# A transformed convolution on one core: other places for two weight loads, another order of the first unit, other copy costs

## The chip, the cores and the metric

The kernel runs on 1 core of one Trainium2 chip. The metric is the device time of one execution in microseconds; the number of a kernel is the median of its runs. TensorE (PE) multiplies, VectorE (DVE) and ScalarE (ACT) read and write PSUM and SBUF, GpSimd (POOL) works on SBUF, and SyncE (SP) issues nearly all transfers on one queue.

## The reference

A convolution along the sequence with three taps, an affine step per output channel, and SiLU. All tensors are bf16.

```python
B, S, C = 2, 2048, 1024          # x: (B, S, C); w: (3, C, C); mean, var, g, b: (C,)
xp = jnp.pad(x, ((0, 0), (1, 1), (0, 0)))
y = sum(jnp.einsum('bsc,cd->bsd', xp[:, k:k + S, :], w[k]) for k in range(3))
y = (y - mean) * (g / jnp.sqrt(var + 1e-5)) + b
return y * sigmoid(y)
```

## The kernel before

Instead of three taps for each row, the kernel uses a transform that gives 6 output rows from 8 input rows with 8 products ("points" 0 to 7). 2048 rows make 342 tiles of 6.

**Input.** The rows of a batch come in 17 windows of 21 tiles (127 or 128 rows, the last one of 33). `load_window` (L203) fetches a window; its tiles are in a pool of 10 buffers, `xwin`, save for the first window of each batch, which has the buffer `xw0`. `transform` (L216) multiplies a window on TensorE with the transform matrix `Rm`, one matmul for each of the 8 blocks of 128 input channels, and copies the result from PSUM to the bf16 tensor `T_sb[batch]`, laid out by channel block, point and tile. In batch 0 a copy holds 4 blocks (672 elements for each partition); in batch 1 a window makes three groups of 3, 3 and 2 blocks (504, 504 and 336), each in one of the PSUM banks 4 to 7 in turn. Each copy goes to ScalarE or VectorE, whichever has less in the running account `load`; `EVAC` (L175) gives a copy's price on each as a fixed part and a part for each block.

**Weights.** They come in 8 chunks of 128 output channels. Points 0 and 7 use the raw taps 0 and 2. The weights of points 1 to 6 are the tensor `uch`, made on GpSimd: `scale_weights` (L142) makes the scaled taps `w2x`, `w1x`, `w0x`; `pair_sum` (L156) adds the outer taps, with `n` = 0, 1, 2 for three weightings; `pair_tap` (L169) adds the middle tap to such a sum or subtracts it from it, for points 1, 3, 5 and 2, 4, 6. So `pair_sum` needs taps 0 and 2 alone, and every `pair_tap` needs tap 1. For chunks 2 to 7, ScalarE does the scaling and VectorE the first sum (`outer_by_reduce`); chunks 2 to 7 come in pairs by `load_weights` (L82), chunks 0 and 1 tap by tap by `load_chunk` (L87), 256 KB each in runs of 256 bytes.

**Units.** A unit (`unit`, L258) is one chunk for one batch: 64 matmuls of 342 columns, 8 for each point, into four banks. bA takes points 1, 2 and 0, bB 3 and 4, bC 5 and 6, bG 7. Points that share a bank accumulate, with copies of the partial sums between them (`copy_out` on ScalarE: m1, m3, s1, s2, m5) and combining steps on VectorE (`stt`, L279). A later point of a bank can't start until the copy of the earlier one is made. Three activations (`silu`) end the unit; they are put off into the next one by the list `late`, and are called from `copy_out`. The order of points is 1, 3, 2, 4, 5, 7, 6, 0; in the first unit, with `seven_first`, it is 7, 1, 3, 2, 4, 5, 0, 6.

**Order.** It is written out by hand: each engine runs its instructions in program order. The loop at L344 runs the windows of batch 0, with the taps of chunk 0 issued behind window 3 (tap 0), 5 (tap 2) and 13 (tap 1), and GpSimd's work for chunk 0 at windows 7 and 13. The loop at L366 runs the windows of batch 1, with chunk 1's taps issued at window 10, and spreads the first 52 matmuls of the first unit (chunk 0, batch 0) between its 51 groups. Then come the rest of the first unit and the other units, with the weights of the next chunk made during the second unit of the chunk before it (L425 to L439). For chunk 1, GpSimd also makes `w2x` (L431). SyncE issues in this order as well.

Of the kernel before, what the change touches and what calls it, by code (L numbers as in the profile page):

```python
# [9 lines left out]
ALU = mybir.AluOpType  # L10
# [25 lines left out]
def kernel(  # L36
# [45 lines left out]
    def load_weights(dp):  # L82
        open_weights(dp)
        for k in (0, 2, 1):
            nc.sync.dma_start(out=pair_tile[dp][:, k], in_=w_all[:, k, :, dp * 2 * P:(dp + 1) * 2 * P])

    def load_chunk(dc, k):  # L87
        nc.sync.dma_start(out=raw[dc][k], in_=w_all[:, k, :, dc * P:(dc + 1) * P])  # L88
# [53 lines left out]
    def scale_weights(dc, taps=(2, 1, 0), on_gpsimd=False):  # L142
        for k in taps:
            f = 2.0 if k == 1 else 4.0
            dst = wx[dc, k] = wtmp.tile([P, CT, P], BF16, name=f"w{k}x")
            if on_gpsimd:
                nc.gpsimd.tensor_scalar(dst, raw[dc][k], f, 0.0, op0=ALU.mult, op1=ALU.add)
            else:
                nc.scalar.mul(dst, raw[dc][k], f)

    def open_chunk(dc):
        wts[dc] = upool.tile([P, 6, CT, P], BF16, name="uch")
# [3 lines left out]
    def pair_sum(dc, n, engine=nc.gpsimd):  # L156

        e = outer[dc, n] = wtmp.tile([P, CT, P], FP32, name=("e1", "e2", "eh")[n])
        a = wx[dc, 0] if n == 2 else raw[dc][0]
        c = wx[dc, 2] if n == 1 else raw[dc][2]  # L160
        engine.tensor_tensor(e, a, c, op=ALU.add)  # L161
# [7 lines left out]
    def pair_tap(dc, n, op):  # L169
        odd = wx[dc, 1] if n else raw[dc][1]  # L170
        nc.gpsimd.tensor_tensor(wts[dc][:, 2 * n + (op == ALU.subtract)], outer[dc, n], odd, op=op)  # L171

    T_sb = [tpool.tile([P, CT, NJ, NTB], BF16, name=f"T_sb{bi}") for bi in range(B)]
    load = {"act": 0.0, "dve": 1.0}
    EVAC = {"act": (0.17, 0.14), "dve": (0.12, 0.17)}  # L175

    sk = consts.tile([P, DC], FP32, name="sk")
    beta = consts.tile([P, DC], FP32, name="beta")
# [59 lines left out]
        else:  # L238
            nc.vector.tensor_copy(dst, src)  # L239

    def mms(bk, j, dc, bi, c0, c1, start):

        for ct in range(CT):
            if j in (0, 7):
                lhsT = raw[dc][0 if j == 0 else 2][:, ct, :]
            else:
                lhsT = wts[dc][:, j - 1, ct, :]
            nc.tensor.matmul(  # L248
                ps_all[:, bk * 512:bk * 512 + c1 - c0],
                lhsT=lhsT,  # L250
                rhs=T_sb[bi][:, ct, j, c0:c1],
                start=start and ct == 0,
                stop=ct == CT - 1,
                skip_group_check=not start,
            )
            yield

    def unit(dc, bi, c0, c1, banks, yT, late, pace=(1, 0, 1, 1, 0), seven_first=False):  # L258

        nn = c1 - c0
        A, B_, C_, G = [ps_all[:, k * 512:k * 512 + nn] for k in banks]
        bA, bB, bC, bG = banks
        pace = list(pace)  # L270

        def et(name):
            return epool.tile([P, NTB], FP32, name=name)[:, 0:nn]

        m1, m3, m5, s1, s2, d1 = (et(n) for n in ("m1", "m3", "m5", "s1", "s2", "d1"))
        y_all = epool.tile([P, M_OUT, NTB], FP32, name="y")[:, :, 0:nn]
        y = [y_all[:, i] for i in range(M_OUT)]

        def stt(o, i0, s, i1, op1=ALU.add):  # L279
            nc.vector.scalar_tensor_tensor(out=o, in0=i0, scalar=s, in1=i1, op0=ALU.mult, op1=op1)  # L280
            load["dve"] += 0.0013 * nn

        def copy_out(dst, src):
            for _ in range(pace.pop(0)):
                if late:
                    late.pop(0)()
            nc.scalar.copy(dst, src)  # L287
            load["act"] += 0.0013 * nn

        if seven_first:  # L290
            yield from mms(bG, 7, dc, bi, c0, c1, True)
        yield from mms(bA, 1, dc, bi, c0, c1, True)
        copy_out(m1, A)
        yield from mms(bB, 3, dc, bi, c0, c1, True)
        copy_out(m3, B_)
        yield from mms(bA, 2, dc, bi, c0, c1, False)
        copy_out(s1, A)
        stt(d1, m1, 2.0, A, op1=ALU.subtract)
        yield from mms(bB, 4, dc, bi, c0, c1, False)
        copy_out(s2, B_)  # L300
        for i in (2, 4):
            stt(y[i], B_, ALPHA * 2.0 ** i, s1)
        stt(B_, m3, 2.0, B_, op1=ALU.subtract)
        yield from mms(bC, 5, dc, bi, c0, c1, True)
        copy_out(m5, C_)
        while late:
            late.pop(0)()
        for i in (1, 3, 5):
            stt(y[i], B_, ALPHA * 2.0 ** i, d1)
        yield from mms(*((bA, 0) if seven_first else (bG, 7)), dc, bi, c0, c1, not seven_first)  # L310
        nc.vector.tensor_tensor(y[5], G, y[5], op=ALU.add)  # L311
        yield from mms(bC, 6, dc, bi, c0, c1, False)
        for i in (2, 4):
            stt(y[i], C_, BETA * 0.5 ** i, y[i])
        stt(G, m5, 2.0, C_, op1=ALU.subtract)
        if not seven_first:
            yield from mms(bA, 0, dc, bi, c0, c1, False)
        for i in (1, 3, 5):
            stt(y[i], G, BETA * 0.5 ** i, y[i])
        stt(y[0], s2, ALPHA, A)  # L320
        stt(y[0], C_, BETA, y[0])

        def silu(i0, i1):
            nc.scalar.activation(  # L324
                yT[:, i0:i1:2, c0:c1],
                y_all[:, i0:i1:2],
                ACT.Silu,
                bias=beta[:, dc:dc + 1],
                scale=sk[:, dc:dc + 1],
            )  # L330

        late.extend(lambda i=i: silu(*i) for i in ((2, 5), (1, 6), (0, 1)))
# [10 lines left out]
    with tc.tile_pool(name="xwin", bufs=10) as xpool:  # L343
        for wi in range(NWIN):  # L344
            window = load_window(xpool, 0, wi)
            if wi in (3, 5, 13):
                load_chunk(0, {3: 0, 5: 2, 13: 1}[wi])
            for h in range(2):
                transform(0, wi, window, 4 * h, 4, (2 * wi + h) % 4 * 2, 2)
            if wi == 0:  # L350
                turn_params()
            if wi == 7:
                open_chunk(0)
                for n, taps in ((0, ()), (1, (2,)), (2, (0,))):
                    scale_weights(0, taps, on_gpsimd=True)
                    pair_sum(0, n)
            if wi == 13:
                pair_tap(0, 0, ALU.add)
                scale_weights(0, (1,), on_gpsimd=True)
                for n, op in ((1, ALU.add), (0, ALU.subtract), (1, ALU.subtract), (2, ALU.add), (2, ALU.subtract)):  # L360
                    pair_tap(0, n, op)
        make_params()
        first = unit(0, 0, 0, NTB, (0, 1, 2, 3), yTs[0], late, seven_first=True)
        load["act"] = load["dve"] = 0.0
        gi, done = 0, 0
        for wi in range(NWIN):  # L366
            window = load_window(xpool, 1, wi)
            if wi == 10:
                for k in (0, 2, 1):
                    load_chunk(1, k)  # L370
            for ct0, n in ((0, 3), (3, 3), (6, 2)):
                transform(1, wi, window, ct0, n, 4 + gi % 4, 3)
                gi += 1
                want = 52 * max(gi - 1, 0) // (3 * NWIN - 1)
                run(first, want - done)
                done = want
        load_weights(1)
        run(first)

# [40 lines left out]
    for ui, (dc, bi) in enumerate(units[1:-1], 1):  # L420
        yT = yTs[ui % 2]
        half = 4 * (ui % 2)
        if bi == 0 and dc + 1 < DC:
            outer_by_reduce(dc + 1)
        if bi == 1 and dc + 1 < DC:  # L425
            open_chunk(dc + 1)
            if dc == 0:
                pair_sum(1, 0)
                for op in (ALU.add, ALU.subtract):
                    pair_tap(1, 0, op)  # L430
                scale_weights(1, (2,), on_gpsimd=True)  # L431
                scale_weights(1, (1, 0))
            else:
                scale_weights(dc + 1)
            for n in range(0 if dc else 1, 3):
                if n:
                    pair_sum(dc + 1, n)
                for op in (ALU.add, ALU.subtract):
                    pair_tap(dc + 1, n, op)  # L439
        run(unit(dc, bi, 0, NTB, (half, half + 1, half + 2, half + 3), yT, late))  # L440
        if ui < len(units) - 2:
            late.append(lambda dc=dc, bi=bi, yT=yT: finish(dc, bi, yT))
        if bi == 1 and dc % 2 == 1 and (dc + 3) // 2 < DC // 2:
            load_weights((dc + 3) // 2)
# [87 lines left out]
```

## Time and profile before

| | us |
|---|---|
| median of 3 runs | 194.63 |
| lowest and highest run | 193.66, 194.88 |
| profiled execution | 193.69 |
| its span | 191.8 |
| TensorE busy | 178.5 |
| VectorE busy | 161.7 |
| GpSimd busy | 147.9 |
| ScalarE busy | 123.3 |

All times in views are microseconds from the start of the span. A row of the timeline gives start, length, engine, line, operation, what it writes and reads, the count, and in brackets the idle time of the engine before it and what ended it. Such rows overlap a little, since instructions are pipelined. In a table of stretches each engine has its busy time with the number of its instructions. The granted TensorE clock is 0.989 over the span.

The groups of batch 1's stage, 21.5 to 39.5 us, that matter here, with the mean length of one (ns):

| engine, line, what | count | mean ns |
|---|---|---|
| ACT L237 copy of 504 | 17 | 605 |
| ACT L237 copy of 336 | 7 | 453 |
| DVE L239 copy of 504 | 15 | 682 |
| DVE L239 copy of 336 | 9 | 506 |
| DVE L280 combining step (y<-ps_all,s) | 2 | 509 |
| ACT L287 copy out of a bank (m<-ps_all) | 3 | 450 |
| POOL L171 weights of a point | 8 | 2127 to 2134 |
| POOL L147 scaling of a tap | 1 | 1037 |

### The profile page before, as it was taken

The numbers are of one execution on the slowest core, as the hardware profiler recorded it, in microseconds if no ns is written. First come the engines' busy times: TensorE is split into PE (matmuls) and PEld (weight loads), VectorE is DVE, ScalarE is ACT, GpSimd is POOL, SyncE is SP. The second block draws the span as 40 slices with busy tenths as digits, with TensorE's granted clock in tenths as the row PEclk, the third lists the DMA queues.
The fourth block names the chain that finished last, engine by engine and source line by source line (L and its number), as shares of the span: only waits on it lengthen the run. The fifth ranks groups of instructions, "written<-read, shape, count | busy, mean of one in ns | idle before, by whom it ended". The sixth has DMA issues, their size and how long they took to land.

```text
span 191.8 us, 3900 instructions
## 1 busy us (share of the span) xinstructions
PE 178.5 (93%) x1404; PEld 125.2 (65%) x1404; DVE 161.7 (84%) x344; ACT 123.3 (64%) x206; POOL 147.9 (77%) x89
## 2 busy tenths in 40 slices
PE   7877799999999999999999999999999999999840
PEld 3666688866666666666666666666666666679830
DVE  6579898987999699969996998799789969697880
ACT  3778588878278628764874587368727782727940
POOL 6379999999949996999699969987997899600000
PEclk9999999999999999999999999999999999999995
DMA  5999999960609398998374699676474738285604
GB/s 133 311 373 316 363 274 241 288 151 8 115 19 190 63 200 224 198 200 174 75 162 87 155 286 214 134 156 123 112 137 96 151 87 164 69 178 122 153 6 109
DMA packets 86759, 31.72 MB, mean 165 GB/s; under 512 B 73364, under 2 KB 82580, under 8 KB 86740
## 3 DMA queue, kind: packets, MB, share of 16 engines
q1 hardware_dynamic: 86637, 31.46, 70.0%
q8 instruction: 11, 0.18, 0.4%
q14 instruction: 8, 0.07, 0.1%
q10 hardware_dynamic: 103, 0.02, 0.0%
HBM read 14.82 MB, written 8.39 MB: 121 GB/s over the span
## 4 chain that ended last, share of the span: by engine, by line
PE 78%; DMA 10%; DVE 5%; ACT 2%; issue 1%; SPq 0%; DVEq 0%; ACTq 0%
PE ps_all L248 74%; DMA xw<-in_x_dram 10%; PE ps_all L223 5%; DVE y L280 3%; ACT yT L324 1%; DVE T_sb L239 1%; DVE o_end L490 1%; DVE ps_all L280 0%; ACT s L287 0%; DVE y L311 0%; DVE o_end L498 0%; ACT m L287 0%; SPq L88 0%; PE ps_all L458 0%; DVEq L490 0%
## 5 line engine op out<-in xcount | busy, mean ns | idle before, releaser
L248 PE MATMUL ps_all<-T_sb,uch 128*128 128x342 bf16 (+2 forms) x816 | 123.4, 299 | 1.1 <-ACT m L287 1.1
L248 PEld LDWEIGHTS <-uch 128*128 128x128 bf16 x816 | 76.6, 97 | 34.9 <-issue 1.5
L324 ACT ACTIVATE yT<-y,beta,sk 128x684 bf16<-128x684 f32 (+8 forms) x51 | 47.1, 926 | 32.0 <-DVE y L280 31.9
L280 DVE SCALAR_TENSOR_TENSOR y<-ps_all,y 128x342 f32<-128x342 f32 (+2 forms) x102 | 45.4, 486 | 1.8 <-PE ps_all L248 0.7
L248 PE MATMUL ps_all<-T_sb,wch 128*128 128x342 bf16 (+2 forms) x272 | 44.1, 299 | 0.0
L171 POOL TENSOR_TENSOR uch<-e,wch 128x1024 bf16<-128x1024 f32 x16 | 33.8, 2133 | 10.5 <-PE ps_all L248 5.6
L171 POOL TENSOR_TENSOR uch<-e,w1x 128x1024 bf16<-128x1024 f32 x16 | 33.8, 2132 | 0.6
L171 POOL TENSOR_TENSOR uch<-eh,w1x 128x1024 bf16<-128x1024 f32 x16 | 33.8, 2134 | 0.5
L287 ACT COPY m<-ps_all 128x342 f32<-128x342 f32 (+2 forms) x51 | 21.6, 425 | 19.6 <-PE ps_all L248 18.9
L223 PE MATMUL ps_all<-Rm,xw 128*128 128x168 bf16 (+1 forms) x272 | 29.7, 238 | 4.1 <-DMA xw<-in_x_dram 3.7
L248 PEld LDWEIGHTS <-wch 128*128 128x128 bf16 x272 | 25.6, 97 | 11.2
L237 ACT CAST T_sb<-ps_all 128x672 bf16<-128x672 f32 (+5 forms) x45 | 26.0, 606 | 8.4 <-PE ps_all L223 7.5
L239 DVE CAST T_sb<-ps_all 128x672 bf16<-128x672 f32 (+3 forms) x40 | 26.4, 698 | 4.0 <-PE ps_all L223 3.5
L223 PEld LDWEIGHTS <-xw 128*128 128x128 bf16 (+1 forms) x272 | 22.2, 100 | 10.1 <-DMA xw<-in_x_dram 5.2
L280 DVE SCALAR_TENSOR_TENSOR y<-ps_all,d 128x342 f32<-128x342 f32 (+2 forms) x51 | 22.0, 485 | 0.6
L280 DVE SCALAR_TENSOR_TENSOR y<-ps_all,s 128x342 f32<-128x342 f32 (+2 forms) x34 | 15.1, 487 | 4.0 <-ACT s L287 4.0
L161 POOL TENSOR_TENSOR e<-wch,w2x 128x1024 f32<-128x1024 bf16 x8 | 17.0, 2126 | 0.2
L161 POOL TENSOR_TENSOR eh<-w0x,wch 128x1024 f32<-128x1024 bf16 x8 | 17.0, 2128 | 0.1
L280 DVE SCALAR_TENSOR_TENSOR d<-m,ps_all 128x342 f32<-128x342 f32 (+2 forms) x17 | 8.3, 487 | 10.4 <-ACT s L287 10.4
L280 DVE SCALAR_TENSOR_TENSOR ps_all<-m,ps_all 128x342 f32<-128x342 f32 (+2 forms) x34 | 16.6, 487 | 0.0
L287 ACT COPY s<-ps_all 128x342 f32<-128x342 f32 (+2 forms) x34 | 14.2, 419 | 0.0
L167 DVE TENSOR_REDUCE e<-wch 128x1024 f32<-128x2048 bf16 x6 | 13.7, 2278 | 0.0
(44 smaller groups left out, 70.2 us busy)
## 6 DMA issues: line engine op xcount, KB each, us to landing
xw<-in_x_dram SPq DMA_DIRECT2D x30, 256.0 KB
out_dram<-o_sb SPq DMA_DIRECT2D x28, 192.0 KB
wch<-in_w_dram SPq DMA_DIRECT2D x9, 512.0 KB
out_dram<-o_sb SPq DMA_DIRECT2D x14, 120.0 KB
wch<-in_w_dram SPq DMA_DIRECT2D x6, 256.0 KB
xw<-in_x_dram SPq DMA_DIRECT2D x2, 224.0 KB
out_dram<-o_before SPq DMA_DIRECT2D x2, 192.0 KB
o_sb<-yT SPq DMA_TRANSPOSE x14
```

The costliest lines, as they stand in the source:

```text
L161: engine.tensor_tensor(e, a, c, op=ALU.add)
L167: nc.vector.tensor_reduce(e, taps.rearrange("p k ct d -> p ct d k"), axis=mybir.AxisListType.X, op=ALU.add)
L171: nc.gpsimd.tensor_tensor(wts[dc][:, 2 * n + (op == ALU.subtract)], outer[dc, n], odd, op=op)
L223: nc.tensor.matmul(banks[:, at:at + NJ * ntile], lhsT=xw[0:kk, (ct0 + c) * P:(ct0 + c + 1) * P], rhs=Rm[0:kk, :, 0:ntile], start=True, sto ...
L237: nc.scalar.copy(dst, src)
L239: nc.vector.tensor_copy(dst, src)
L248: nc.tensor.matmul(ps_all[:, bk * 512:bk * 512 + c1 - c0], lhsT=lhsT, rhs=T_sb[bi][:, ct, j, c0:c1], start=start and ct == 0, stop=ct == C ...
L280: nc.vector.scalar_tensor_tensor(out=o, in0=i0, scalar=s, in1=i1, op0=ALU.mult, op1=op1)
L287: nc.scalar.copy(dst, src)
L324: nc.scalar.activation(yT[:, i0:i1:2, c0:c1], y_all[:, i0:i1:2], ACT.Silu, bias=beta[:, dc:dc + 1], scale=sk[:, dc:dc + 1],)
L490: nc.vector.tensor_copy(ends[k][0:n1 - n0], pv[0:n1 - n0])
```

## The change

It has four parts, all before the third unit.

- The taps of chunk 0 are issued elsewhere on SyncE's queue: tap 2 behind window 6, tap 0 behind window 10, tap 1 behind the last window of batch 0. GpSimd's work for chunk 0 stands in one piece, in the order w2x, sum 0, sum 1, w0x, point 1, w1x, points 3, 2, 4, sum 2, points 5, 6. It is the same 12 instructions.
- The first unit's order is 0, four of the eight matmuls of 7, then 1, 3, 2, 4, 5, the other four of 7, and 6. The first 12 of its matmuls run before the windows of batch 1, and 40 are spread between the groups. Point 0 starts bank A, so points 1 and 2 accumulate on it: ScalarE copies out m0 and a0 instead of s1 and s2, and VectorE takes m0 off again in two combining steps (s1 and A) that were not there. `y[0]` gets its part of point 0 earlier. VectorE has two instructions more in this unit and ScalarE's copies are as many as before.
- Chunk 1's taps are issued behind all windows of batch 1. Its `w2x` is made by ScalarE, not GpSimd.
- The prices of `EVAC` have smaller fixed parts. By the account that follows from them, ScalarE gets 19 copies of 504 (or their short ones) and 10 of 336 in batch 1, VectorE 15 and 7; before, it was 19 and 8 against 15 and 9.

```diff
-    EVAC = {"act": (0.17, 0.14), "dve": (0.12, 0.17)}
+    EVAC = {"act": (0.09, 0.14), "dve": (0.085, 0.17)}
...
-        if seven_first:
-            yield from mms(bG, 7, dc, bi, c0, c1, True)
-        yield from mms(bA, 1, dc, bi, c0, c1, True)
-        copy_out(m1, A)
+        if not zero_first:
+            yield from mms(bA, 1, dc, bi, c0, c1, True)
+            copy_out(m1, A)
+        else:
+            m0, a0 = et("m0"), s2
+            yield from mms(bA, 0, dc, bi, c0, c1, True)
+            copy_out(m0, A)
+            yield from mms(bG, 7, dc, bi, c0, c1, True, range(CT // 2))
+            yield from mms(bA, 1, dc, bi, c0, c1, False)
+            copy_out(m1, A)
         yield from mms(bB, 3, dc, bi, c0, c1, True)
         copy_out(m3, B_)
         yield from mms(bA, 2, dc, bi, c0, c1, False)
-        copy_out(s1, A)
+        if not zero_first:
+            copy_out(s1, A)
+        else:
+            copy_out(a0, A)
+            stt(s1, A, 1.0, m0, op1=ALU.subtract)
+            stt(A, A, 1.0, m0)
         stt(d1, m1, 2.0, A, op1=ALU.subtract)
         yield from mms(bB, 4, dc, bi, c0, c1, False)
-        copy_out(s2, B_)
+        if not zero_first:
+            copy_out(s2, B_)
+        else:
+            stt(y[0], B_, ALPHA, a0)
...
-        yield from mms(*((bA, 0) if seven_first else (bG, 7)), dc, bi, c0, c1, not seven_first)
+        yield from mms(bG, 7, dc, bi, c0, c1, not zero_first, range(CT // 2 if zero_first else 0, CT))
...
-            if wi in (3, 5, 13):
-                load_chunk(0, {3: 0, 5: 2, 13: 1}[wi])
+            if wi in (6, 10, NWIN - 1):
+                load_chunk(0, {6: 2, 10: 0, NWIN - 1: 1}[wi])
...
-            if wi == 7:
-                open_chunk(0)
-                for n, taps in ((0, ()), (1, (2,)), (2, (0,))):
-                    scale_weights(0, taps, on_gpsimd=True)
-                    pair_sum(0, n)
-            if wi == 13:
-                pair_tap(0, 0, ALU.add)
-                scale_weights(0, (1,), on_gpsimd=True)
-                for n, op in ((1, ALU.add), (0, ALU.subtract), (1, ALU.subtract), (2, ALU.add), (2, ALU.subtract)):
-                    pair_tap(0, n, op)
+        open_chunk(0)
+        scale_weights(0, (2,), on_gpsimd=True)
+        pair_sum(0, 0)
+        pair_sum(0, 1)
+        scale_weights(0, (0,), on_gpsimd=True)
+        pair_tap(0, 0, ALU.add)
+        scale_weights(0, (1,), on_gpsimd=True)
+        pair_tap(0, 1, ALU.add)
+        for n in (0, 1):
+            pair_tap(0, n, ALU.subtract)
+        pair_sum(0, 2)
+        for op in (ALU.add, ALU.subtract):
+            pair_tap(0, 2, op)
         make_params()
-        first = unit(0, 0, 0, NTB, (0, 1, 2, 3), yTs[0], late, seven_first=True)
+        first = unit(0, 0, 0, NTB, (0, 1, 2, 3), yTs[0], late, zero_first=True)
         load["act"] = load["dve"] = 0.0
-        gi, done = 0, 0
+        gi, done = 0, 12
+        run(first, done)
         for wi in range(NWIN):
             window = load_window(xpool, 1, wi)
-            if wi == 10:
-                for k in (0, 2, 1):
-                    load_chunk(1, k)
             for ct0, n in ((0, 3), (3, 3), (6, 2)):
                 transform(1, wi, window, ct0, n, 4 + gi % 4, 3)
                 gi += 1
-                want = 52 * max(gi - 1, 0) // (3 * NWIN - 1)
+                want = 12 + 40 * max(gi - 1, 0) // (3 * NWIN - 1)
                 run(first, want - done)
                 done = want
+        for k in (0, 2, 1):
+            load_chunk(1, k)
         load_weights(1)
         run(first)
...
-                scale_weights(1, (2,), on_gpsimd=True)
-                scale_weights(1, (1, 0))
+                scale_weights(1)
```

## The prediction

> **What bounds the kernel now.** I read the page first (share of each engine, the 40 slices), then the chain of waits, then TensorE's, GpSimd's and ScalarE's rows in order of time for the first 45 us, and the table of stretches for the DMA rates.
>
> ```profile
> span 191.8 us, 3900 instructions
> ...
> PE 178.5 (93%) x1404; PEld 125.2 (65%) x1404; DVE 161.7 (84%) x344; ACT 123.3 (64%) x206; POOL 147.9 (77%) x89
> ...
> PE   7877799999999999999999999999999999999840
> ...
> PE 78%; DMA 10%; DVE 5%; ACT 2%; issue 1%; SPq 0%; DVEq 0%; ACTq 0%
> ```
>
> TensorE is full from the sixth slice (24 us) to the tail; only the first five slices have room. So the change is worth what it takes from the time before TensorE is full, less any new wait behind it. The rows of TensorE show the edges of that stretch:
>
> ```profile
> 11.41 5.97 PE L223 MATMUL ps_all<-Rm,xw 128*128 128x168 bf16 x64 [1.00 <-DMA xw<-in_x_dram]
> 18.04 0.75 PE L223 MATMUL ps_all<-Rm,xw 128*128 128x168 bf16 x8 [0.66 <-DMA xw<-in_x_dram]
> 19.12 1.08 PE L223 MATMUL ps_all<-Rm,xw 128*128 128x168 bf16 x16 [0.32 <-DMA xw<-in_x_dram]
> 21.50 0.59 PE L223 MATMUL ps_all<-Rm,xw 128*128 128x168 bf16 x6 [1.30 <-DMA xw<-in_x_dram]
> ```
>
> The first batch is through at 20.20; then 1.30 us of idling until batch 1's first window lands (the chain has that transfer from 14.78 for 6.59 us: landed at 21.37). Two rates of the queue, and the stage after it (last columns: clock, DMA share, GB/s):
>
> ```profile
> 10.50:14.50 4.00, 3.02 (x35) 2.59 (x36) 2.91 (x4) 2.98 (x5) 3.51 (x3) 1.00 1.05 387
> 26.00:29.00 3.00, 3.00 (x36) 2.57 (x34) 2.81 (x5) 2.57 (x6) 3.00 (x2) 1.00 1.06 217
> 21.50:39.50 18.00, 17.90 (x188) 14.73 (x189) 16.25 (x32) 15.13 (x33) 17.84 (x10) 1.00 1.03 285
> ```
>
> In 10.5 to 14.5 x rows travel alone: a window of 128 rows (262 KB) takes 0.68 us at 387 GB/s. In 26 to 29 it is mostly chunk 1's taps: the same bytes take 1.2 us at 217. A tap ahead of the windows costs 1.2 us of queue.
>
> **Before, in fixed points.** S = 21.50: batch 1's windows begin. E = 39.51: its 136 transform matmuls and 52 of the unit's 64 are done (row at 39.22, two more of 0.145). X = 43.77: the second unit's third tap starts, after a wait for ScalarE's copy; from there the chain is TensorE without a break (31.23 us for 214 matmuls), so any shift of X goes through to the end. The stage S to E is 18.0 us. Its work: 128 transforms in threes of 0.22 (9.3) and 8 short ones (0.4), 52 matmuls of 0.145 (7.5), together 17.2; 0.8 is stalls, mainly these VectorE pieces of the chain:
>
> ```profile
> 35.63 0.68 DVE T_sb L239
> 36.31 0.85 DVE y L280 x2
> ```
>
> **Part 1: middle tap behind batch 0, first 12 matmuls ahead of batch 1.** With 1.2 us less in the queue the first batch is through at about 19.0; it cannot come before 18.0, because the copies set 0.75 us a window (5.97 us for eight) from 5.98 on. The 12 matmuls need its last copy (before: last copy at 21.03, 0.83 after TensorE; I take 0.7), so they run from 19.7 to 21.4 (12 x 0.145). The bytes ahead of batch 1's first window are the same as before, only in another order, so it still lands at about 21.4 and S stays 21.5, now with 12 matmuls done in what was idling: 1.74 us. If the first batch gains nothing, they end at 22.7 and 1.2 of this is lost.
>
> The Trainium skill ("DMA: Bandwidth & Descriptors", section "Why small descriptors are slow") charges a 256-byte descriptor 3 cycles on 8; a tap would then cost about 0.9 us, an estimate from that page, against the 1.2 of the rows. By it the 12 matmuls end at 21.7 instead of 21.4, still before the wait of part 2, and the sum is the same.
>
> **Part 2: GpSimd's chain starts later.** This is the new wait. Its rows now:
>
> ```profile
> 10.84 2.12 POOL L161 TENSOR_TENSOR e<-wch 128x1024 f32<-128x1024 bf16 x1 [2.78 <-DMA wch<-in_w_dram]
> ...
> 19.56 2.12 POOL L171 TENSOR_TENSOR uch<-e,wch 128x1024 bf16<-128x1024 f32 x1
> 21.65 1.04 POOL L147 TENSOR_SCALAR w1x<-wch 128x1024 bf16<-128x1024 bf16 x1
> 22.77 2.13 POOL L171 TENSOR_TENSOR uch<-e,w1x 128x1024 bf16<-128x1024 f32 x1
> ```
>
> The steps are 2.09 (tensor) and 1.12 (scale). Everything from the first weight of point 1 on needs the middle tap, which lands at L. Batch 1's first window is behind it (0.67 us), so L is at most 20.7. The last window of batch 0 had landed by 19.1 to 19.9; without the tap ahead 17.9 to 18.7, and 1.2 for the tap gives 19.1 to 19.9 as the lower end. I take 20.4, nearer the upper end, since the queue's total is what the trace shows. Then point 1's weights are ready at L+2.1 = 22.5, while TensorE is there at 21.5 + three groups (0.6) = 22.1: a wait of 0.4, with the windows queued behind it on TensorE. Point 3's are ready at L+5.3 = 25.7; TensorE comes at 22.5 + 8 x 0.145 + 10 groups of 0.193 = 25.6. Points 2, 4 and 5 (L+7.4, L+9.5, L+13.8, the sum with four more tensor steps and a pair sum) are ready at 27.8, 29.9, 34.2, before TensorE at 28.8, 31.9, 35.0. What is left after 25.7: 32 matmuls (4.6) and 38 groups, three of them short (7.2): E would be 37.5.
>
> **Part 3: the copies.** Back-to-back instructions overlap by 0.09 (two of VectorE's 0.51 in 0.93). By that the stage holds on VectorE 15 copies of 504 (0.59), 7 of 336 (0.42) and 7 combining steps (0.42) = 14.7; on ScalarE 19 (0.52), 10 (0.36) and 3 unit copies (0.36) = 14.6. The two extra combining steps (s1 and A) and the new weights of the copies are in that. Before it was 14.3 and 14.6 in 18.0 us; now it has to fit in 16. The bursts of three and four steps on VectorE hold copies behind them, and four banks are all the room. Bounds: no stall, or, with full durations and no overlap (17.4 us), E = 39.9, 2.4 more. I take 0.5, below the 0.8 of before, as the cost weights move copies off VectorE just there. E = 38.0.
>
> **Part 4: chunk 1's weights behind batch 1, its scaling on ScalarE.** The three taps no longer stand before windows 11 to 16; the 0.15 us late matmul at 32.83 goes. They are issued when batch 1's sixth window frees its buffer (about 28) and land by 33.5; GpSimd wants them at L+15.9 = 36.3, so their later place costs nothing. ScalarE now has three scalings where it had two:
>
> ```profile
> 39.46 1.06 ACT L149 ACTIVATE w1x<-wch 128x1024 bf16<-128x1024 bf16 x1
> 40.42 1.05 ACT L149 ACTIVATE w0x<-wch 128x1024 bf16<-128x1024 bf16 x1
> 42.43 0.96 ACT L324 ACTIVATE yT<-y,beta,sk 128x684 bf16<-128x684 f32 x1 [0.97 <-DVE y L280]
> 43.30 0.99 ACT L287 COPY m<-ps_all 128x342 f32<-128x342 f32 x2
> ```
>
> After E: copy 0.45, three scalings of 0.96, activation 0.87, copy 0.45, then the third tap: X = E + 4.65. Before it was E + 4.26: 0.4 us given back. For GpSimd, chunk 1 ends at 36.3 + 19.4 = 55.7 (before 33.21 to 53.7, less one scaling); the third unit wants its fifth and last weights at 54.3 and 56.6 (start 49.6 + 32 or 48 x 0.145), ready at 53.6 and 55.7. Slack 0.7: no wait, but little room. SyncE's later transposes wait for ScalarE as before and shift with it.
>
> **Sum.** X = 38.0 + 4.65 = 42.65 against 43.77: 1.1 us less. The profiled execution took 193.69 (span 191.8 and 1.9 around it), so 192.6 by its own time; that execution lies 0.94 under the median of the timed runs, 194.63 (193.66 to 194.88), so in medians 193.5. One per cent is 1.95 us, about what a measurement here can tell.
>
> **Rivals.** (A) The middle tap lands by 19.7 and GpSimd is never waited for: E = 22.1 + 14.9 = 37.0 with 0 to 0.5 of copy stalls, X 41.6 to 42.1, gain 1.6 to 2.1: 192.8. For it: rates show room; against: the queue's total. (B) Slower: VectorE and ScalarE become the bound of the stage. With full durations E = 39.9, X = 44.5: 0.8 slower, 195.4; it loses from E = 39.1 on. If GpSimd's chunk 1 then also misses the third unit, 1 to 2 us more (L over 21.1 uses up the slack of 0.7): 197. For it: both engines at 95% of the stage; against: the same work gave 0.8 of stalls at 81%. (C) Nothing to see: the tap lands at 21.4 with the first window, GpSimd takes back the 12 matmuls' gain: 194.5.
>
> **Numbers.** Forecast 0.5, A 0.2, B 0.13, C 0.17. Range from A without stalls (gain 2.1, 192.5) to B (195.4), with about half of the timed runs' own spread (1.2) added below and a little above: 192.0 to 195.6. Faster by over 1%: A's better half and the forecast's lucky edge, 0.2; slower by over 1%: B with the missed unit, 0.07; the rest within.
>
> **What would show it.** Twelve unit matmuls between 19.5 and 21.6 and the first window of batch 1 at about 21.5; a TensorE wait for GpSimd's uch of 0.3 to 0.6 near 22; the end of batch 1's stage near 38; a wait for ScalarE's copy of 0.6 near 42. Wrong if the first batch is not through by 19.5, if the waits for T_sb copies exceed 1 us, or if TensorE waits for GpSimd again after 50.

## The result, and the profile after

| | us |
|---|---|
| changed kernel, median of 4 runs | 196.82 (195.98 to 197.95) |
| before, beside it, median of 4 runs | 194.19 (193.66 to 194.88) |
| ratio, with its 95% interval | 1.014 (1.0094 to 1.0186) |
| changed kernel, profiled execution | 196.13, span 194.2 |

The change made the kernel 1.4% slower; 0.6% faster was forecast. First the page of the changed kernel: span, busy shares, slices, chain, and one group of the costliest instructions.

```profile
span 194.2 us, 3920 instructions
...
PE 179.3 (92%) x1404; PEld 125.3 (65%) x1404; DVE 160.4 (83%) x343; ACT 125.2 (65%) x210; POOL 146.9 (76%) x88
...
PE   7777699999999999999999999999999999999940
...
PE 78%; DMA 8%; DVE 6%; ACT 3%; issue 1%; SPq 1%; DVEq 0%; ACTq 0%
...
L248 PE MATMUL ps_all<-T_sb,wch 128*128 128x342 bf16 (+2 forms) x272 | 42.7, 300 | 1.6 <-DVE sk L195 1.6
```

The line of slices is as full as before from the sixth on, and its fifth slice (19.4 to 24.3 us) has fallen from 7 to 6. The share of DMA in the chain is smaller, those of VectorE and ScalarE are larger. The group of unit matmuls with raw taps has an idle time that before did not have: 1.6 us, ended by VectorE's `sk`. TensorE's rows in order of time show where:

```profile
12.51 2.92 PE L223 MATMUL ps_all<-Rm,xw 128*128 128x168 bf16 x32 [1.03 <-DMA xw<-in_x_dram]
16.43 2.99 PE L223 MATMUL ps_all<-Rm,xw 128*128 128x168 bf16 x32 [1.00 <-DMA xw<-in_x_dram]
19.70 1.07 PE L223 MATMUL ps_all<-Rm,xw 128*128 128x168 bf16 x16 [0.28 <-DMA xw<-in_x_dram]
22.37 1.90 PE L248 MATMUL ps_all<-T_sb,wch 128*128 128x342 bf16 x12 [1.61 <-DVE sk L195]
24.11 0.74 PE L223 MATMUL ps_all<-Rm,xw 128*128 128x168 bf16 x8
```

Batch 0 is through at 20.77 (before 20.20). The 12 matmuls are there, but start at 22.37, and batch 1's windows begin behind them at 24.11 (S, before 21.50): no longer because of a transfer, which had landed by then, but because TensorE itself comes late. The chain of waits of the changed kernel has the stretch between:

```profile
20.82 0.33 ACT T_sb L237
...
21.33 0.35 DVE T_sb L239
21.68 0.08 DVE sc L192
...
21.79 0.18 DVE beta L193
...
21.99 0.17 DVE beta L194
22.15 0.08 DVE sk L195
...
22.37 1.90 PE ps_all L248 x12
```

The four steps of `make_params` (L191) read `prmT`, which `turn_params` (L186) has put into the last 16 columns of bank 0 behind the first window. They are issued behind batch 0 and ahead of the first unit. Before, that unit began with point 7 in bank 3, and nothing waited for them. Now it begins with point 0 in bank A, which is bank 0, and its first matmul waits until the last reader of `prmT` is done, though it writes columns 0 to 341.

Then the stage of batch 1 in the table of stretches (last columns: clock, DMA share, GB/s):

```profile
24.11:41.48 17.37, 16.88 (x178) 13.56 (x176) 15.53 (x30) 14.60 (x33) 17.13 (x10) 1.00 0.98 270
```

It takes 17.37 us with 40 unit matmuls in it; before it took 18.0 with 52. Twelve matmuls fewer (1.74 us) have shortened it by 0.6. The chain says who sets its length late in the stage:

```profile
34.62 0.61 ACT T_sb L237
35.23 0.34 ACT s L287
...
35.59 0.52 DVE s L280
36.11 0.44 DVE ps_all L280
...
36.57 0.38 DVE d L280
...
37.00 0.69 DVE T_sb L239
...
38.14 0.68 DVE T_sb L239
```

ScalarE copies a window, then the unit's a0 (the tile `s`); VectorE can take m0 off only then, in the two steps that the change adds (`s`, `ps_all`), and behind them and d1 stands a window's copy that TensorE needs for a free bank.

Behind the stage ScalarE's rows in order of time answer to those of before:

```profile
42.03 1.06 ACT L149 ACTIVATE w2x<-wch 128x1024 bf16<-128x1024 bf16 x1
42.99 1.05 ACT L149 ACTIVATE w1x<-wch 128x1024 bf16<-128x1024 bf16 x1
43.94 1.05 ACT L149 ACTIVATE w0x<-wch 128x1024 bf16<-128x1024 bf16 x1
44.88 0.94 ACT L341 ACTIVATE yT<-y,beta,sk 128x684 bf16<-128x684 f32 x1
45.73 0.78 ACT L287 COPY m<-ps_all 128x342 f32<-128x342 f32 x2
```

Three scalings stand where two stood, and the second unit's third tap starts at X = 46.22, 4.74 after E = 41.48 (before: 4.26). Last, GpSimd's first point:

```profile
21.21 2.13 POOL L171 TENSOR_TENSOR uch<-e,wch 128x1024 bf16<-128x1024 f32 x1
```

It starts as soon as the scaling ahead of it ends, so the middle tap had landed; its weights are ready at 23.34, and TensorE first asks for them near 24.7. The forecast wait is not there, because TensorE is later.

So X moved by 46.22 − 43.77 = +2.45, and the span by 2.4. Against the forecast X of 42.65 it is +3.57: S comes 2.61 late, the stage takes 17.37 where 16.5 was forecast (+0.87), and the piece from E to X is 0.09 longer than forecast. The 2.61 has two parts: batch 0 is through at 20.77 where 19.0 was forecast (1.77 late), and the wait behind it is 1.61 where 0.7 was forecast (0.91 more); 0.1 of their sum was room ahead of S.

### The profile page after: what moved, and what is told of

Read it like the earlier page. It is cut to its first block, busy times and chain, and to the rows that moved or that the text cites. A ratio compares the mean times of both kernels' runs of the same rounds, so it can differ in the third digit from the quotient of the medians.

```text
span 194.2 us, 3920 instructions
## 1 busy us (share of the span) xinstructions
PE 179.3 (92%) x1404; PEld 125.3 (65%) x1404; DVE 160.4 (83%) x343; ACT 125.2 (65%) x210; POOL 146.9 (76%) x88
## 4 chain that ended last, share of the span: by engine, by line
PE 78%; DMA 8%; DVE 6%; ACT 3%; issue 1%; SPq 1%; DVEq 0%; ACTq 0%
PE ps_all L248 73%; DMA xw<-in_x_dram 8%; PE ps_all L223 4%; DVE y L280 2%; DVE T_sb L239 2%; ACT yT L341 1%; PE ps_all L477 1%; SPq L213 1%; ACT T_sb L237 1%; ACT w2x L149 1%; DVE o_end L509 1%; ACT w1x L149 0%; DVE ps_all L280 0%; ACT s L287 0%; ACT w0x L149 0%
## 5 line engine op out<-in xcount | busy, mean ns | idle before, releaser
L248 PE MATMUL ps_all<-T_sb,wch 128*128 128x342 bf16 (+2 forms) x272 | 42.7, 300 | 1.6 <-DVE sk L195 1.6
L223 PE MATMUL ps_all<-Rm,xw 128*128 128x168 bf16 (+1 forms) x272 | 28.8, 239 | 3.6 <-DMA xw<-in_x_dram 3.1
L237 ACT CAST T_sb<-ps_all 128x672 bf16<-128x672 f32 (+5 forms) x48 | 26.8, 612 | 7.2 <-PE ps_all L223 6.5
L239 DVE CAST T_sb<-ps_all 128x672 bf16<-128x672 f32 (+4 forms) x37 | 24.2, 694 | 7.3 <-PE ps_all L223 7.0
L223 PEld LDWEIGHTS <-xw 128*128 128x128 bf16 (+1 forms) x272 | 21.7, 100 | 10.0 <-DMA xw<-in_x_dram 5.0
L280 DVE SCALAR_TENSOR_TENSOR y<-ps_all,s 128x342 f32<-128x342 f32 (+2 forms) x35 | 15.6, 487 | 4.2 <-ACT s L287 4.2
## 6 DMA issues: line engine op xcount, KB each, us to landing
out_dram<-o_sb SPq DMA_DIRECT2D x28, 192.0 KB
out_dram<-o_before SPq DMA_DIRECT2D x2, 192.0 KB
```

Of the source, the lines that this page charges most:

```text
L223: nc.tensor.matmul(banks[:, at:at + NJ * ntile], lhsT=xw[0:kk, (ct0 + c) * P:(ct0 + c + 1) * P], rhs=Rm[0:kk, :, 0:ntile], start=True, sto ...
L248: nc.tensor.matmul(ps_all[:, bk * 512:bk * 512 + c1 - c0], lhsT=lhsT, rhs=T_sb[bi][:, ct, j, c0:c1], start=start and ct == 0, stop=ct == C ...
```

## Experiments

The theory after this: (1) the place of the parameter steps, by the wait for them, is what made the kernel slower; (2) the gain forecast for the stage went into the copies and the combining steps queued with them. Rivals: other parts of the change, the clock, TensorE's own work, GpSimd.

### The wait for the parameter steps

**e1_params_early**: the changed kernel with its parameter steps in the loop of batch 0.

```diff
             if wi == 0:
                 turn_params()
+            if wi == 8:
+                make_params()
...
-        make_params()
```

> The changed kernel with VectorE's four small parameter steps (make_params) behind window 8 instead of behind batch 0. Theory W (the first unit matmul waits for these steps, because they read the bank that point 0 writes): the wait of TensorE for sk (1.6 us in the changed kernel) shrinks by 0.5 to 0.6 us, and the time falls by about 0.6 us to 196.2. Theory C (the copies set the length of batch 1's stage, so an earlier start is lost again there): the wait shrinks but the stage's end moves by less than 0.2 us, time within 0.2 us of the changed kernel.

Measured: median 193.58, ratio to before 0.9994 (0.997 to 1.0017). TensorE's rows of this kernel:

```profile
14.38 5.01 PE L223 MATMUL ps_all<-Rm,xw 128*128 128x168 bf16 x56 [0.95 <-DVE sk L195]
19.88 1.90 PE L248 MATMUL ps_all<-T_sb,wch 128*128 128x342 bf16 x12 [0.49 <-ACT T_sb L237]
21.61 0.74 PE L223 MATMUL ps_all<-Rm,xw 128*128 128x168 bf16 x8
```

The wait ahead of the 12 matmuls is now 0.49 and for a window's copy, they lie where the forecast had them, and S is 21.61. The whole loss is gone, far more than the 0.6 us that was expected; the forecast gain is not there either (E = 39.21, X = 43.94). The steps' wait hasn't vanished, it has moved: the first row has 0.95 for `sk`. There TensorE makes up for it: the 56 matmuls behind it run without a break and batch 0 is through at 19.39.

S is 2.50 earlier than in the changed kernel, in two parts. The wait is 1.12 shorter, not just by the 0.55 that the four steps take: in the changed kernel they also stand behind VectorE's last copy (done at 21.68), while in e1 the unit starts at 19.88, as soon as ScalarE's copy is made, and VectorE's ends at 20.30. The other 1.38 is batch 0 itself, through at 19.39 instead of 20.77. The place of the steps is thus shown to cost the time, but only the 1.12 is shown to be the wait.

**e2_w2x_gpsimd**: one other part undone, chunk 1's `w2x` back on GpSimd.

```diff
-                scale_weights(1)
+                scale_weights(1, (2,), on_gpsimd=True)
+                scale_weights(1, (1, 0))
```

> The changed kernel with chunk 1's w2x made by GpSimd again. Theory S (ScalarE's three scalings in a row hold the second unit's first copy): the second unit's third tap starts 4.2 to 4.3 us after the end of batch 1's stage instead of 4.7, the time falls by 0.4 to 0.5 us. Rival (GpSimd's chain for chunk 1, now 3 to 4 us later than before, has no room): GpSimd ends chunk 1 1.1 us later, TensorE waits for uch in the third unit, and the time does not fall or rises by up to 0.7.

Measured: 195.19, ratio 1.0039 (0.9994 to 1.0084). X − E is 4.37, so the scaling on ScalarE was worth 0.37. The median lies 1.6 us under the changed kernel's, more than that can give; its ten runs spread from 194.01 to 198.41, with mean clocks of 0.993 down to 0.971. The profiled execution (196.85) shows a second effect, in TensorE's row of the 12 matmuls:

```profile
21.95 3.52 PE L248 MATMUL ps_all<-T_sb,wch 128*128 128x342 bf16 x12 [1.60 <-DVE sk L195]
```

and in the table of stretches of the same kernel (the last three columns are the granted clock, DMA share and GB/s):

```profile
21.86:25.27 3.41, 3.32 (x12) 1.79 (x13) 0.00 (x0) 0.44 (x1) 3.33 (x3) 0.50 1.06 386
```

At half the clock the same 12 matmuls took 3.52 us instead of 1.90, after an idle time of the same 1.60. The clock fell at 21.86, 1.52 us into that idle time.

**e3_taps_before**: chunk 0's taps and GpSimd's work for them as before, all else as changed.

```diff
-            if wi in (6, 10, NWIN - 1):
-                load_chunk(0, {6: 2, 10: 0, NWIN - 1: 1}[wi])
+            if wi in (3, 5, 13):
+                load_chunk(0, {3: 0, 5: 2, 13: 1}[wi])
...
+            if wi == 7:
+                open_chunk(0)
...
+            if wi == 13:
+                pair_tap(0, 0, ALU.add)
...
```

> The changed kernel with chunk 0's taps behind windows 3, 5 and 13 and GpSimd's work for chunk 0 at windows 7 and 13, as before. Theory D (the new order of taps itself makes the windows late: batch 0 was through at 20.77 instead of 20.20): batch 0 is through by 20.2 and the time falls by 0.5 us or more. Theory W/C (it is not the taps): batch 0 is through at 20.2 or later, TensorE's start of batch 1 stays within 0.4 us of 24.3, the time stays within 0.4 us of the changed kernel.

Measured: 196.78, ratio 1.0138 (1.0066 to 1.0209), like the changed kernel. The wait is there too, and the profiled execution (198.01) has a clock of 0.50 for 6.83 us, from 20.46 to 27.29:

```profile
19.34 1.07 PE L223 MATMUL ps_all<-Rm,xw 128*128 128x168 bf16 x16 [0.43 <-DMA xw<-in_x_dram]
21.93 3.60 PE L248 MATMUL ps_all<-T_sb,wch 128*128 128x342 bf16 x12 [1.51 <-DVE sk L195]
...
20.46:27.29 6.83, 5.36 (x25) 3.62 (x26) 2.53 (x8) 1.38 (x4) 6.75 (x5) 0.50 0.86 313
```

Batch 0 is through at 20.41, so the clock fell when the wait for `sk` had hardly begun: in this execution that wait can't be the reason. The place of the taps is not what made the change slower.

**e4_old_unit_order**: the first unit's old order (7, 1, 3, 2, 4, 5, 0, 6, with 52 matmuls spread), the other parts as changed.

```diff
-        first = unit(0, 0, 0, NTB, (0, 1, 2, 3), yTs[0], late, zero_first=True)
+        first = unit(0, 0, 0, NTB, (0, 1, 2, 3), yTs[0], late, seven_first=True)
...
-        gi, done = 0, 12
-        run(first, done)
+        gi, done = 0, 0
...
-                want = 12 + 40 * max(gi - 1, 0) // (3 * NWIN - 1)
+                want = 52 * max(gi - 1, 0) // (3 * NWIN - 1)
```

> The changed kernel with the first unit in its old order (7, 1, 3, 2, 4, 5, 0, 6, with 52 matmuls spread over batch 1's groups); taps, chunk 1's loads, w2x on ScalarE and the copy prices stay changed. Theory C with W (the 12 matmuls ahead, the denser stage and the two extra combining steps cost more than the idle time they fill): the stage's stalls fall from 1.7 to under 1.0 us and the time falls by 1 to 2 us, to 195 to 196. Theory D (taps): it stays at 196.5 or above, since the windows are as late as in the changed kernel.

Measured: 195.52, ratio 1.0053 (1.0013 to 1.0093). No matmul waits for `sk`, but TensorE idles 1.43 us for batch 1's first window, and the profiled execution has a clock of 0.50 from 21.19 to 28.02 (0.32 us into the idle time). Its two runs with a mean clock of 0.987 took 193.37 and 193.81, like the kernel before; the eight with 0.974 to 0.982 took 195.22 to 197.12. So the order of the unit doesn't explain everything that these kernels lose: the clock can fall at this place with or without the wait for `sk`.

**e5_filler** and **e11_filler_short**: the changed kernel with matmuls of zeros in the wait, into columns of bank 7 that nobody reads; 40 of them in e5, 28 in e11.

```diff
         gi, done = 0, 12
+        for _ in range(40):
+            nc.tensor.matmul(ps_all[:, 7 * 512 + 424:7 * 512 + 496], lhsT=warm[:, 0:P], rhs=warm[:, 0:72], start=True, stop=True)
         run(first, done)
```

> The changed kernel with 40 small matmuls of zeros (72 columns, into columns that nobody reads) between batch 0's last window and the first unit matmul; the wait for VectorE's parameter steps stays. Theory K (the clock: TensorE idles in that wait, and in some executions its granted clock then falls to 0.5 for 3.4 or 6.8 us, as it did at 21.9 and 20.5 in two of the runs before): no stretch at half clock before the tail, runs within about 1 us of each other, the time falls by 1 to 2 us to 194.7 to 195.7, though the wait itself is as long. Rival (the wait alone costs the time, the clock is beside the point): the time stays at 196 or above.

> The changed kernel with 28 matmuls of 72 zero columns into an unused corner of a bank, ahead of the first unit's matmul, so that they end inside the wait for the parameter steps (about 1.0 of the 1.6 us idle). The order of all other work and the wait stay. Theory of the clock (the idle stretch lets the granted clock fall in some executions): no profiled half clock before the tail, and the runs lie within 0.5 us of one another around 195.2 to 195.5, under the changed kernel's runs of 196.0 to 198.0. Rival (the clock plays no part, the wait alone costs): median 196.0 to 197 with the same spread as the changed kernel.

**e12_changed_again**: the changed kernel, in the same set of runs as e11.

> The changed kernel itself beside the three others, so that its spread is seen over ten runs. Theory of the clock: two groups of runs, one near 195.2 to 196.1 (no fall of the clock) and one 1.5 to 2 us above it, median 195.5 to 197; the profile shows 0.5 of the full clock for 3.4 or 6.8 us near 21 if it belongs to the upper group. Rival (one wait of fixed length): one group within 0.6 us.

Measured: e5 195.6 (195.47 to 195.79, four runs), ratio 1.0088 (1.0058 to 1.0117), although its filler ends about half a microsecond after the parameter steps. e11 195.18 (194.41 to 197.61, twelve runs), ratio 1.0077 (1.0042 to 1.0112). e12 196.37 (194.85 to 197.29, six runs), ratio 1.011 (1.0064 to 1.0157). In e5 and e11 the filler itself starts only when a copy has left bank 7 free, as TensorE's rows of e11 show:

```profile
20.10 1.07 PE L387 MATMUL ps_all<-warm 128*128 128x72 bf16 x28 [0.62 <-DVE T_sb L239]
21.00 1.91 PE L248 MATMUL ps_all<-T_sb,wch 128*128 128x342 bf16 x12
22.75 0.74 PE L223 MATMUL ps_all<-Rm,xw 128*128 128x168 bf16 x8
```

Beside each timed run stands its mean granted clock:

| kernel | runs with a mean clock of 0.987 or more | runs below |
|---|---|---|
| e12_changed_again | 194.85, 195.41 | 196.34, 196.4, 196.64, 197.29 (0.983 to 0.986) |
| e11_filler_short | nine, 194.41 to 195.6 | 196.99, 197.24, 197.61 (0.982 to 0.984) |
| e5_filler | four, 195.47 to 195.79 | none |

A stretch of 3.41 us at half clock lowers the mean over 194 us by 0.5 x 3.41 / 194 = 0.009, the step between the columns. So the clock plays a part, against the rival of e11 and e12; but the short filler did not keep the runs together as the theory expected: in three of twelve the clock was low all the same. No profile fell on such a run of e11, so what lowered it there stays open. With the steps early, 61 of 62 runs (e1 and e6 to e10) have a clock of 0.987 or more; the other has 0.986.

A low clock is not new with the change, however. Of the 79 runs of the kernel before that were taken beside e1 to e12, 46 have a mean of 0.987 or more (median 193.66), 15 have 0.982 to 0.986 and are no longer (median 193.42), and 18 have 0.981 or less and took 194.35 to 196.67. So the mean alone doesn't tell whether a stretch at half clock cost time, and the kernel before, which has no wait for `sk`, loses time with a low clock as well.

The Trainium skill ("TensorE: Matmul & The Clock Gate", sections "What's actually happening" and "HAM oscillation — how this bites in real kernels") describes a clock that is either full or half, decided in windows of about 3.4 us, and warns of idle gaps longer than that. The two levels and the lengths of 3.41 and 6.83 us agree with these rows. The warning doesn't: no idle gap ahead of these falls was longer than 1.6 us, and the clock fell 1.52 (e2), 0.05 (e3) and 0.32 us (e4) into one. In the 3.41 us ahead of the fall TensorE was busy for 1.07, 1.91 and 1.53 us; in the profile of e12, which shows no fall, it was busy for 1.07 of the 3.41 us ahead of the unit. So these rows give no rule for when the clock falls.

### The stage of batch 1

To see what stretches the stage, I added up what lies between the starts of successive matmuls over their own length (0.145 for one of a unit, 0.073 for one of a full window, 0.05 for one of the last), by what released the later one:

| kernel | unit matmuls in the stage | S to E | lost | of it to VectorE's copies | ScalarE's copies | GpSimd's weights | other |
|---|---|---|---|---|---|---|---|
| before | 52 | 18.0 | 0.81 | 0.43 | 0 | 0 | 0.38 |
| changed | 40 | 17.37 | 1.94 | 1.05 | 0.56 | 0 | 0.34 |
| e1 | 40 | 17.6 | 2.15 | 0.98 | 0.56 | 0.27 | 0.34 |
| e6 | 40 | 17.45 | 2.02 | 1.12 | 0.56 | 0 | 0.34 |
| e9 | 40 | 16.42 | 0.96 | 0.44 | 0 | 0.07 | 0.45 |
| e10 | 46 | 18.02 | 1.66 | 0.30 | 0.42 | 0.61 | 0.34 |

(E is counted here as the end of the stage; a copy's column holds the wait for the bank that it frees.)

**e6_params_and_w2x**: e1 and e2 together, the base of the next ones.

> Parameter steps behind window 8, and chunk 1's w2x on GpSimd. Theory S (ScalarE's third scaling gives back 0.4 to 0.5 us): the second unit's third tap starts 4.3 us after the end of batch 1's stage instead of 4.7, and the time is 0.3 to 0.5 below the kernel with the parameter steps alone (193.58), about 193.1. Rival (GpSimd has no room for it): TensorE waits for uch in the third unit, 193.6 or above.

Measured: 193.6, ratio 0.9991 (0.9971 to 1.0011); X − E = 4.38, E = 39.20. By the profile the third scaling is worth 0.35 at X; in the medians (193.58 with it, 193.6 without) it can't be seen.

**e7_params_old_prices**: e1 with the old prices of the copies.

```diff
-    EVAC = {"act": (0.09, 0.14), "dve": (0.085, 0.17)}
+    EVAC = {"act": (0.17, 0.14), "dve": (0.12, 0.17)}
```

> Parameter steps behind window 8, and the copies priced as before. If the new prices help (copies moved off VectorE where it has its bursts), batch 1's stage is 0.2 to 0.6 us longer than with the parameter steps alone and the time 193.8 to 194.2. If they make no difference or hurt, it is 193.6 or below.

Measured: 193.81, ratio 0.9992 (0.997 to 1.0014); S to E takes 17.5 (e1 17.6). The time lies in the range expected if the prices help, but beside the runs of the kernel before the two kernels are equal (0.9992 and 0.9994). The prices make no difference that these runs show.

**e8_seven_ahead**: the old order of the first unit with point 7's eight matmuls ahead of batch 1 and 44 spread; early steps, `w2x` on GpSimd, taps and prices as changed. It has neither m0 nor the two added combining steps.

```diff
-        gi, done = 0, 12
+        gi, done = 0, 8
...
-                want = 12 + 40 * max(gi - 1, 0) // (3 * NWIN - 1)
+                want = 8 + 44 * max(gi - 1, 0) // (3 * NWIN - 1)
```

> The taps, chunk 1's loads and the copy prices of the changed kernel, parameter steps behind window 8, w2x on GpSimd, but the first unit in its old order with the 8 matmuls of point 7 ahead of batch 1 and 44 spread over its groups, so without the two extra combining steps. Theory C (the extra steps and the bursts behind them set the stalls of the stage): the stage's end comes 0.5 to 1.0 us earlier than with the parameter steps alone (39.2), the time is 192.3 to 193.0, below both kernels. Rival (the stage is limited by the sum of the copies): its end stays at 39.0 or later and the time at 193.2 or above.

Measured: 194.41, ratio 1.0031 (1.0012 to 1.005); S to E takes 18.74, of which 0.47 is waiting for GpSimd's weights, wanted earlier in this order, and 1.8 for copies. So the added steps are not all of the copies' cost: without them the stage is no shorter. (It also has four more matmuls in it than e6, 0.58 us, and another order.)

**e9_narrow_copies**: e6 with half the columns in batch 1's copies. It leaves out half of batch 1's transformed data, and batch 1's units read batch 0's.

```diff
         dst = T_sb[bi][:, ct0:ct0 + n, :, WT * wi:WT * wi + ntile]
+        if bi:
+            src, dst = src[:, :, 0:NJ // 2], dst[:, :, 0:NJ // 2]
...
-                rhs=T_sb[bi][:, ct, j, c0:c1],
+                rhs=T_sb[0][:, ct, j, c0:c1],
```

> The kernel with early parameter steps and w2x on GpSimd (span 191.5, batch 1's stage 21.75 to 39.20 = 17.45 us, TensorE's own work in it about 15.5), with one thing taken out: batch 1's copies bring only four of the eight rows of j (252 or 168 columns instead of 504 or 336), and the units of batch 1 read batch 0's T_sb, so that batch 1's outputs are those of batch 0. Every matmul, weight step, transfer and combining step stays. Theory (the copies and the combining steps queued with them set the length of this stage): with half the copied columns the waits for T_sb go, the stage takes 15.5 to 16.0 us, its end comes at 37.3 to 37.8 and the time at 191.8 to 192.3. Rival (the lost 2 us are TensorE's own, its short matmuls and switches between transforms and unit matmuls, or GpSimd's weights): the stage stays at 17.2 to 17.5 and the time at 193.4 to 193.8.

Measured: 193.01, ratio 0.9949 (0.992 to 0.9979). The stage in the table of stretches, of this kernel

```profile
21.46:37.88 16.42, 16.30 (x178) 13.48 (x176) 11.23 (x30) 10.22 (x33) 16.18 (x9) 1.00 1.01 303
```

and of its base e6:

```profile
21.75:39.20 17.45, 16.96 (x178) 13.56 (x176) 15.54 (x30) 14.61 (x33) 17.21 (x10) 1.00 1.04 302
```

The same 178 matmuls, with VectorE and ScalarE busy for 11.2 and 10.2 us instead of 15.5 and 14.6, take 1.03 us less. That is half of what the stage loses, and most of what the copies cost it (1.68 to 0.44 in the table of losses). What remains is 0.44 before VectorE's copies, so the stage is 0.4 longer than the theory had it and ends just above its range, at 37.88; it is far from the rival's. The time gained less than the stage, since TensorE now comes 0.25 us too early for GpSimd's weights in the third unit.

**e10_spread_46**: if copies set the stage, more matmuls fit into it for less than their own length. e6 with 46 spread.

```diff
-                want = 12 + 40 * max(gi - 1, 0) // (3 * NWIN - 1)
+                want = 12 + 46 * max(gi - 1, 0) // (3 * NWIN - 1)
```

> The kernel with early parameter steps and w2x on GpSimd, with 46 instead of 40 of the first unit's matmuls spread between batch 1's transforms (58 of 64 done when the stage ends, six more of 0.145 = 0.87 us). Theory (copies set the stage, not TensorE): the stage takes the 17.45 us of before plus at most one VectorE step of 0.42, so the second unit starts 0.4 to 0.9 earlier than at 41.07; ScalarE's two scalings (until 41.76) then hold the second unit's third tap back, which starts at 43.1 to 43.4 instead of 43.58; time 193.0 to 193.5. Rival (TensorE sets the stage): it takes 0.87 longer, the second unit starts at 41.0 to 41.2, time 193.6, no change.

Measured: 192.87 (192.53 to 194.12, twelve runs), ratio 0.9951 (0.9922 to 0.9981): faster than the kernel before by half a per cent, and than the changed one by nearly 2%. Six more matmuls of 0.87 us made the stage 0.57 us longer, most of it for GpSimd's weights, wanted earlier; the waits for copies fell from 1.68 to 0.72. The second unit starts at 40.64 instead of 41.07. ScalarE's rows of this kernel show what is next:

```profile
40.81 1.05 ACT L149 ACTIVATE w0x<-wch 128x1024 bf16<-128x1024 bf16 x1
41.80 0.96 ACT L341 ACTIVATE yT<-y,beta,sk 128x684 bf16<-128x684 f32 x1
42.67 0.99 ACT L287 COPY m<-ps_all 128x342 f32<-128x342 f32 x2
```

The two scalings run into the activation without a gap, and the second unit's third tap starts at 43.14, as expected, behind the first of the two copies.

## Why the prediction was wrong

**Fixed points and the shift of X.** Right: X moved by 2.45 and the span by 2.4; X and the span of the other profiled executions move together as well (e1 43.94 and 191.9, e10 43.14 and 191.1).

**Part 1, the 12 matmuls: this step failed.** "The 12 matmuls need its last copy (… I take 0.7)" named one wait and left out another: by the new order the unit's first matmul goes to bank 0, whose last columns the parameter steps still read. It measured 1.61, and 0.49 with the steps moved. The prediction went through the copies and the transfers, and never through the small instructions that stand between batch 0 and the unit in program order.

The step ahead of it failed as well, and by more: "the first batch is through at about 19.0". In the changed kernel's two profiles it was through at 20.77 and 20.18 (e12), against 20.20 before, so the queue's 1.2 us did not come out as time. In the first of them, 15 of the 16 completions of a window's transfer came close together and the last 1.1 to 1.5 us later, from the fifth window on. With the steps early, batch 0 is through at 19.2 to 19.5, the matmuls run from 19.88 to 21.61 (19.7 to 21.4 forecast) and S is 21.61 (21.5). But e11, with the steps late, has 19.48 too, so why batch 0 is late in some executions stays open.

**The clock.** Not in the prediction at all. Half the clock for 3.41 us cost 1.62 us on the 12 matmuls of e2 (3.52 against 1.90); by the runs beside e12 it is part of the changed kernel's median, not of its profile. Between the changed kernel's two medians and e1's lie 2.8 to 3.2 us. About 1 of it is the wait: e11 and e1 have batch 0 through at nearly the same time (19.48 and 19.39), and X is 44.85 against 43.94; the medians of their runs with a clock of 0.987 or more are 194.71 and 193.58. The rest is the clock and batch 0's lateness, which runs and profiles don't separate.

**Part 2, GpSimd.** The wait of 0.4 did not come in the changed kernel, since TensorE was late. GpSimd's first point was late as well: it started at 21.21 behind GpSimd's own earlier steps, a bound that the prediction did not have. With TensorE in time (e1) the wait came, smaller: 0.27; there the point started at 20.17, behind the middle tap (20.4 forecast). The third unit did not wait for chunk 1's weights.

**Part 3, the copies: the mis-sized term.** Between its bounds of 0 and 2.4, "I take 0.5" was too small. The stage lost 1.94 us where 0.9 was forecast (0.5, and 0.4 of GpSimd), 1.61 of it before copies. The mechanism is rival B's, in part: not that the two engines are full (15.5 and 14.6 busy of 17.4), but that a copy stands behind unit copies and combining steps that wait for each other. e9 shows it by narrowing the copies, e10 by filling the gaps. The reason given for the small value, that the cost weights move copies off VectorE, has no weight: the old prices (e7) do as well. The sums for VectorE were short too: before, 14.3 is what four combining steps make, where the trace has six that start in the stage, and 14.7 counts seven, where it has eight.

**Part 4, ScalarE's scaling.** Right: 4.74 for 4.65 forecast (4.26 before).

**Rivals.** A's mechanism, TensorE never waiting for GpSimd, was there, but as a consequence of its being late; its time was not. B named the copies and was right on them, and would have given 195.4; the time is beyond that because of what came ahead of the stage, which no rival had: the wait, batch 0's lateness and the clock. Both of the prediction's own signs of being wrong came: batch 0 not through by 19.5, and more than 1 us of waiting for copies. C's mechanism did not happen. The range (192.0 to 195.6) missed the time by 1.2 us.

Where the expected gain went: 12 matmuls into the idle stretch ahead of S ran where they were forecast once the steps were out of their way (e1), but of their 1.74 us 1.3 were lost again in the stage (17.6 with 40 matmuls against 18.0 with 52), where gaps before copies took their place, and 0.5 at ScalarE (4.73 against 4.26). What the change could give came out only when six more matmuls were put into those gaps.

## What to carry to other kernels

Before another tile is made the first user of a bank, list every instruction that still reads any part of that bank, the small ones too, and see where they stand in program order. A stage in which copies free the banks need not shorten by as much as the matmuls taken out of it (1.74 us taken out gave 0.6 here); put as many into it as its gaps hold, and watch what they need earlier. Here the granted clock fell around a sparse stretch in some executions and not in others; look at the granted clock of several runs of both kernels, not at one profile.

## What was not expected of the hardware

- The granted clock was 0.50 for 3.41 us (e2) or 6.83 us (e3, e4), from 1.52, 0.05 and 0.32 us into idle stretches of 1.60, 1.51 and 1.43 us on; the profile of e12 has such a stretch (1.60) and no fall.
- The last completion of a transfer can be late by 1.1 to 1.5 us against the 15 others for most of a batch, in one execution and not in another. In the six kernels with the new place of the taps and the steps behind batch 0, the profiles have batch 0 through at 19.5 to 20.9; in the six with early steps at 19.2 to 19.5. Late steps alone don't bring it: e5 and e11 have them, and their last completions in batch 0 are 0.4 us late at most.
- Narrowing a copy from 504 to 252 columns in 17 windows took 4.3 us off VectorE's busy time and 4.4 off ScalarE's, and only 1.03 off the stage.
